# The hidden gradient for two slabs at a time, in matmuls of 512 columns, with the taps broadcast by quarters and a sixth gate/up tile

## The chip, the cores and the metric

The kernel runs on one core of a Trainium2 chip. Its time is the device time of one execution in microseconds (us). The engines are named as in the profile: PE is TensorE (PEld its weight loads), DVE is VectorE, ACT is ScalarE, POOL is GpSimd and SP is SyncE, which here only issues DMAs. Each engine works through its own queue in order; they wait for one another by semaphores.

## What is computed

Inputs are bf16: q, k, v and the incoming gradient of 2048 × 1024 (S × D), four shift taps a channel, a filter of 2048 taps a channel (ssm_k), and weights w_gate and w_up (1024 × 3584) and w_down (3584 × 1024). The forward part, cut to what matters:

```
xn = layernorm(q)
kv = shift(k, taps) * v
y  = irfft(rfft(kv) * rfft(ssm_k)) + kv * ssm_D
s  = xn * y
g  = silu(((xn @ w_gate) * (xn @ w_up)) @ w_down)
out = q + s * g
```

The kernel returns out and its gradients for q, k, v, the taps, ssm_k, ssm_D and the three weights. Two of the backward products matter below. With dbm the gradient of the down projection's result, the hidden gradient is dh = dbm @ w_downᵀ (2048 × 3584); it is multiplied by gate and by up, elementwise, to give the gradients of up and gate, and these give dw_gate and dw_up = xnᵀ @ (…).

## The kernel before

**Stages.** Up to about 500 us: the gate and up matmuls (line 671) with the forward convolution beside them. To about 700: the down projection (L1034) with the backward of the silu gate, row block by row block. From 700 to 1317: dh and dw, the stage that the change is about. Then the gradient of w_down (L1582) to 1506, and the gradient of xn (L1644) to the end.

**The dh/dw stage.** The 3584 hidden columns are cut in NSL = 14 slabs of SLW = 256. For one slab there are two half tiles (first and second 1024 rows), each a tile of 1 MB that holds gate and up for 8 row blocks of 128: `[P, a, b, f]` with a = gate/up, b = row block, f = 256 columns. `gu_in` (L1342) loads them from GUd; `U[(11, 6, 2, 3, 12)[k % 5]]` are the five rooms in which they go round. U is the list of large work tiles of 8 KB a partition.

- `dh_half` (L1471) computes dh for one half tile. For each of 8 row blocks it runs 8 matmuls of 256 columns (L1482, one for each dc, the 128-row piece of D), with w_downᵀ of the slab as the moving operand. Two row blocks share one psum tile of 512 columns; ScalarE copies it to `dht` (L1484). After four row blocks a `multiply` is put on the list todo: VectorE multiplies gate and up of four row blocks by `dht` in place. After the second the whole tile is stored to DGd.
- `dw_slab` (L1495) computes dw_gate and dw_up of one slab in 8 groups (dc), each 16 matmuls of 512 columns (L1499; the moving operand is 256 columns of gate and 256 of up), a copy to `wb` (L1504), and after each second group two stores. After each group it takes one step of `others`, which is dh of the next slab: four steps, behind the groups 0 to 3.
- `load_wdt` (L1328) loads w_downᵀ of a slab, by a transposing DMA on SP's queue, into a pool `bw` of two buffers; it is called behind group 3 for the slab after next.
- `after_group` runs what is on todo and then `btick`, which lets a pump issue the next piece of the convolution's backward part: VectorE, ScalarE and POOL work that is spread over the stage and its successors, in proportion to the matmuls issued.

**Order of queues.** The program's order within an engine is that of the calls, except that a scheduler may move an instruction that has no data wait ahead; `tc.issue_after` and PIN hold some in place. SP issues the loads of this stage (gate/up tiles, w_downᵀ, the h tiles and the DBM tiles for the next stage) and the stores of wb and DGd; POOL issues the convolution's transfers and, behind slabs 1 to 4, four transfers that add q to out in memory.

**The taps.** The four shift taps, broadcast to all partitions, are read by VectorE in the forward shift (`shift(dp)`, L759, for four quarters dp of 256 channels) and in the backward units `dk_units` (L1204, 16 units of 128 channels and half the rows) in the last stage. They lie in `Wbc`, a tile of 8 KB a partition that lives through the whole kernel. WTd is the transposed taps in memory. `st` and `cld` are helpers that issue a transfer on POOL's queue, `ld` one on SP's.

Of the kernel before, what the change touches and what calls it, by code (L numbers as in the profile page):

```python
# [13 lines left out]
BF16 = mybir.dt.bfloat16  # L14
# [5 lines left out]
def build_kernel(  # L20
# [11 lines left out]
    nc = tc.nc  # L32
# [92 lines left out]
    nc.scalar.activation(warm[:], warm[:], ACT.Sqrt)  # L125
    RSTD = const.tile([P, NB], F32, name="RSTD")
    RSTN = const.tile([P, NB], F32, name="RSTN")
    Wbc = const.tile([P, 4, D], BF16, name="Wbc")

    tip = tc.alloc_tile_pool(name="tip", bufs=1)  # L130
    TI = tip.tile([P, 2, 8, 2, P], BF16, name="TI")
# [9 lines left out]
    def load_bcast(bsb):  # L141

        wrow = bsb.tile([1, D, 4], BF16, name="wrow")
        st(wrow[:].rearrange("p d j -> p (d j)"), A_shift_k.rearrange("(o d) j -> o (d j)", o=1))
        wtap = bsb.tile([1, 4, D], BF16, name="wtap")

        def turn(j):
            nc.gpsimd.tensor_copy(wtap[:, j, :], wrow[:, :, j])

        def spread():  # L150
            st(WTd.rearrange("(o x) -> o x", o=1), wtap[:].rearrange("p j d -> p (j d)"))
            st(Wbc[:].rearrange("p j d -> p (j d)"), bass.AP(WTd.tensor, WTd.offset, [[0, P], [1, 4 * D]]))
        return turn, spread

    def angles(tg):
# [378 lines left out]
    Dz = kst.tile([P, D], BF16, name="Dz")  # L534
    V.memset(Dz[:], 0.0)
    krow = kst.tile([P, 2, 11, 256], BF16, name="k")
    V.memset(krow[0:1, 0, 0:3, :], 0.0)
    bsb = pool("bc_sb", 1)
    tg = pool("tg", 1)
# [200 lines left out]
    def conv_forward():  # L740
        S_ = conv_state

        def load_kv(dp, c):
            S_["k", dp] = krow
            if dp > 0 or c == 0:
                for i in range(2) if dp == 0 else (c,):
                    cld_k(krow[:, i], i, dp)
            if dp > 0 or c == 1:
                for i in range(2) if dp == 0 else (c,):
                    v = U[4][:, 2048 * i:2048 * i + 2048].rearrange("p (a x) -> p a x", a=8)  # L750
                    cld_v(v, i, dp * 256, 256)
# [6 lines left out]
        def shift(dp):  # L758
            kv = cx.tile([P, NB, 256], BF16, name="kv")  # L759
            S_["kvt", dp] = kv  # L760
            k = S_.pop(("k", dp))
            wb = lambda j: Wbc[:, j:j + 1, dp * 256:(dp + 1) * 256].unsqueeze(1).to_broadcast([P, 2, 8, 256])
            room = cx.tile([P, 16, 256], BF16, name="KX")[:].rearrange("p a x -> p (a x)") if dp == 0 else U[7][:]
            acc, prod, v = [t.rearrange("p (c r d) -> p c r d", c=2, r=8) for t in (U[6][:], room, U[4][:])]
            with tc.issue_after(last.ins):
                tt(acc, k[:, :, 0:8, :], wb(3), MUL)
            yield 2.3
            for j in (2, 1, 0):
                tt(prod, k[:, :, 3 - j:11 - j, :], wb(j), MUL)
# [300 lines left out]
    while conv_state["filters"]:  # L1070
        bm_first([fc_])
        fc_ += 1
    bw = pool("bw", 2, side="right")
    mh = [pool("mh0", 1, side="right")]
    ps_bx = pool("ps_bx", 1, space=PSUM)

# [127 lines left out]
    def dk_units(ew):  # L1204
# [9 lines left out]
        def load_turned(i):  # L1214
# [7 lines left out]
                nc.sync.dma_start_transpose(out=dkT[:], in_=DKSHd[ds, c * H:c * H + H, :])  # L1222
            return kT, dkT

        dk = load_rows(0)
        yield 3
        for i in range(16):
            ds, c = divmod(i, 2)
            dsl = slice(ds * P, (ds + 1) * P)
            wb = lambda j: Wbc[:, j:j + 1, dsl].to_broadcast([P, 8, P])  # L1230
            acc = ew.tile([P, 8, P], BF16, name="dka")
            tt(acc[:], dk[:, 3:11, :], wb(3), MUL)
            for j in (2, 1, 0):
# [92 lines left out]
            defer(turn)  # L1326

    def load_wdt(sl):  # L1328
        wdt = bw.tile([P, DC, SLW], BF16, name="wdt")
        wdt_ld[0] = nc.sync.dma_start_transpose(out=wdt[:], in_=B_w_down[sl * SLW:(sl + 1) * SLW, :])  # L1330
        return wdt

    def load_ht(bp):
        ht = mh[bp % 2].tile([P, NF, 256], BF16, name="ht")
# [1 line left out]
            last = ld(ht[:, f0:f1], ht_rows(bp, f0, f1))  # L1336
        return (lambda fc: ht[:, fc]), last

    DGU = {}
    wdts = []  # L1340
# [12 lines left out]
    room = [bw.tile([P, DC, SLW], BF16, name="wdt")[:].rearrange("p (i x) f -> p i (x f)", i=2) for i in range(2)]  # L1353
# [61 lines left out]
    for bp in range(2, 8):  # L1415
# [6 lines left out]
        with tc.issue_after(row_ld[0].ins):  # L1422
            if bp in (4, 5, 7):
                q = (4, 5, 7).index(bp)
                dma_t = nc.sync.dma_start_transpose(out=DBMT[q], in_=DBMd[512 * q:512 * q + 512, :])
            if bp == 6:
                wdts.append(load_wdt(0))
                dma_t = wdt_ld[0]
        with tc.issue_after(dma_t.ins) if dma_t is not None else nullcontext():
            rows_in[2 * bp + 1] = gate_rows(2 * bp + 1)  # L1430
        if bp > 5:
            with tc.issue_after(row_ld[0].ins):
                gu_in(0) if bp == 6 else wdts.append(load_wdt(1))
        for i in range(2):
            n = (2 * bp + i - 2) * NF
            while done < n + NF:
# [11 lines left out]

    XN = [u8(q, a=4) for q in (7, 0, 1, 9)]
    bg = pool("bg", 2, side="right")  # L1450
    U.append(bg.tile([P, 4096], BF16, name="U12", bufs=1))
    ps_b = ps_tr = pool("ps_b", 4, space=PSUM)
    tr_name[0] = "psb"
    ps_c3 = pool("ps_c3", 2, space=PSUM)
# [13 lines left out]
            todo.pop(0)()  # L1468
        btick(n)

    def dh_half(k, wdt):  # L1471

        sl, hf = divmod(k, 2)
        dgu = DGU[k]
        for g in range(2):
            dht = bg.tile([P, 4, SLW], BF16, name="dht", bufs=3)
            for e in range(2):
                ps = ps_b.tile([P, 512], F32, name="psb")
                for x in range(2):
                    b = 4 * g + 2 * e + x  # L1480
                    for dc in range(DC):
                        nc.tensor.matmul(ps[:, x * SLW:(x + 1) * SLW], DBMT[2 * hf + g][:, dc, (b % 4) * P:(b % 4 + 1) * P],  # L1482
                                         wdt[:, dc, :], start=(dc == 0), stop=(dc == DC - 1))
                nc.scalar.copy(out=dht[:, 2 * e:2 * e + 2].rearrange("p b f -> p (b f)"), in_=ps[:])  # L1484
# [45 lines left out]
    PIN[0] = PINQ[0] = True  # L1530
    for k in range(2):
        run(dh_half(k, wdts[0]))
    todo.pop()()
    for sl in range(NSL):
        if sl + 1 == NSL:
            load_h(0)
            for q in range(4):
                ld(DBM[q], DBMd[512 * q:512 * q + 512, :].rearrange("(b u) d -> u b d", u=P))
            load_h(1)

        def halves():
            for k in (2 * sl + 2, 2 * sl + 3):
                if k < 2 * NSL:
                    yield from dh_half(k, wdts[sl + 1])
# [263 lines left out]
```

## Time and profile before

| | |
|---|---|
| time, median of 3 runs (from to) | 1912.02 us (1911.76 to 1912.31) |
| the profiled execution, its time | 1911.63 us |
| its span in the profile | 1909.9 us |
| granted TensorE clock | 1.00 |
| dh, 1792 matmuls (L1482), first and last | 700.1 to 1273.6 us |
| transposing loads of w_downᵀ (14), issue, shortest/median/longest | 1.7 / 4.9 / 12.8 us |
| the same, issue to landing, shortest/median/longest | 4.2 / 9.3 / 21.7 us |
| gate/up tile load, 1 MB (28), issue to landing, median | 9.3 us |

A line of the group view reads: line, engine, operation, output and input, shape, count, busy time in us, mean in ns of one, and the idle time of the engine before them. A line of the waits view reads: engine and its instruction, the instruction waited for, then total us, number of waits and the longest. The profile's mean of a matmul (273 ns for 256 columns, 379 for 512) includes its pipelined end, which lies beside the next matmul.

### The profile page before, as it was taken

What the parts mean: (1) busy time and instruction counts of PE and PEld (TensorE: products, weight loads), DVE (VectorE), ACT (ScalarE), POOL (GpSimd) and SP (SyncE); (2) the same over time, 40 slices, a digit from 0 to 9 for tenths busy, and PEclk for the clock granted to TensorE, in tenths of its full rate; (3) what the DMA queues carried; (4) which work ended last, traced back from release to release, by engine and by line L of the source; (5) the groups of instructions that cost most, each with busy time, mean ns of one, the idle gap of its engine ahead of it and who ended that gap; (6) DMA issues with size and microseconds to landing.
All of it is one profiled execution on the core that took longest, in us unless ns stands there. A gap on an engine that the chain in (4) does not pass through costs nothing.

```text
span 1909.9 us, 28150 instructions
## 1 busy us (share of the span) xinstructions
PE 1899.4 (99%) x11379; PEld 1013.9 (53%) x11379; DVE 1549.7 (81%) x1711; ACT 636.8 (33%) x927; POOL 332.7 (17%) x465
## 2 busy tenths in 40 slices
PE   8999999999999999999999999999999999999999
PEld 5555555545444466666666665664444444444444
DVE  8999999999988556887999999999995305788862
ACT  5765555556333233432222222222222102111121
POOL 5121211201113220001031221211212101111120
PEclk9999999999999999999999999999999999999999
DMA  9777766769769997677897798585887999989852
GB/s 298 269 263 233 251 208 223 252 211 311 241 227 307 316 314 231 209 231 233 264 277 247 231 266 258 184 286 180 230 238 181 219 206 190 194 187 190 194 166 88
DMA packets 425106, 444.34 MB, mean 233 GB/s; under 512 B 268400, under 2 KB 342796, under 8 KB 410512
## 3 DMA queue, kind: packets, MB, share of 16 engines
q1 hardware_dynamic: 367504, 239.03, 45.9%
q0 software_dynamic: 41152, 174.15, 29.0%
q10 hardware_dynamic: 16320, 29.36, 4.1%
q8 instruction: 89, 1.46, 0.3%
q14 instruction: 41, 0.34, 0.1%
HBM read 193.87 MB, written 189.84 MB: 201 GB/s over the span
## 4 chain that ended last, share of the span: by engine, by line
PE 97%; DVE 1%; ACT 1%; DMA 0%; issue 0%; SPq 0%; ACTq 0%
PE psb L1499 20%; PE psx L1644 20%; PE psg L671 19%; PE psb L1482 10%; PE psbm L1034 10%; PE psb L1582 9%; PE psF L234 3%; PE psI L455 1%; PE tr L565 1%; PE psY L1193 1%; PE psY L445 1%; PE psx L1582 1%; DVE bst L578 0%; DMA wslab<-in_B_w_gate_dram 0%; PE tr L788 0%; DVE U L212 0%
## 5 line engine op out<-in xcount | busy, mean ns | idle before, releaser
L671 PE MATMUL psg<-wslab,U 128*128 128x512 bf16 x1792 | 401.8, 379 | 3.5 <-DMA wslab<-in_B_w_gate_dram 2.1
L1499 PE MATMUL psb<-U,U 128*128 128x512 bf16 x1792 | 397.1, 379 | 0.0
L1644 PE MATMUL psx<-U,dgut 128*128 128x512 bf16 x1536 | 332.8, 379 | 0.0
L1644 PEld LDWEIGHTS <-dgut 128*128 128x128 bf16 x1792 | 175.3, 98 | 211.4
L1499 PEld LDWEIGHTS <-U 128*128 128x128 bf16 x1792 | 175.2, 98 | 198.0
L671 PEld LDWEIGHTS <-U 128*128 128x128 bf16 x1792 | 172.6, 98 | 197.2 <-issue 3.6
L1482 PE MATMUL psb<-wdt,U 128*128 128x256 bf16 x1792 | 205.6, 273 | 0.0
L1482 PEld LDWEIGHTS <-U 128*128 128x128 bf16 x1792 | 175.2, 98 | 29.2
L212 DVE TENSOR_TENSOR W<-W 128x1024 f32<-128x1024 f32 (+1 forms) x189 | 186.5, 1003 | 4.1
L1582 PE MATMUL psb<-U,U 128*128 128x512 bf16 x816 | 177.3, 379 | 0.0
L1504 ACT CAST wb<-psb 128x512 bf16<-128x512 f32 x112 | 65.6, 586 | 315.4 <-PE psb L1499 310.5
L1249 DVE SCALAR_TENSOR_TENSOR dkp<-dkT,kT 128x1024 bf16<-128x1024 bf16 (+2 forms) x64 | 78.3, 1223 | 93.1 <-DMA dkT<-DKSHd 91.4
L1034 PE MATMUL psbm<-U,ht 128*128 128x512 bf16 x672 | 146.0, 379 | 0.0
L1582 PEld LDWEIGHTS <-U 128*128 128x128 bf16 x896 | 87.4, 98 | 104.4
L673 ACT CAST gut<-psg 128x512 bf16<-128x512 f32 x156 | 91.5, 589 | 120.2 <-PE psg L671 119.7
L1676 ACT ACTIVATE dx_t<-dxn 128x1024 bf16<-128x1024 f32 x15 | 15.9, 1057 | 324.7 <-DVE dxn L212 324.7
L1034 PEld LDWEIGHTS <-ht 128*128 128x128 bf16 x672 | 65.7, 98 | 78.1
L212 DVE TENSOR_TENSOR U<-U,dht 128x2048 bf16<-128x2048 bf16 x56 | 68.3, 1220 | 46.5 <-ACT dht L1484 46.5
L1484 ACT CAST dht<-psb 128x512 bf16<-128x512 f32 x112 | 65.6, 587 | 116.4 <-PE psb L1482 116.4
L66 POOL DMA_DIRECT2D Hd<-hN x54 | 36.6, 677 | 268.9 <-DVE hN L212 258.9
L1623 ACT CAST wbs<-psb 128x512 bf16<-128x512 f32 x51 | 29.9, 586 | 145.4 <-PE psb L1582 134.3
L212 DVE TENSOR_TENSOR W<-SP 128x1024 f32<-128x1024 f32 x64 | 74.1, 1218 | 1.3 <-ACT SP L295 0.8
(263 smaller groups left out, 2342.9 us busy)
## 6 DMA issues: line engine op xcount, KB each, us to landing
U<-GUd SPq DMA_DIRECT2D x28, 1024.0 KB, 9.3
DGd<-U SPq DMA_DIRECT2D x28, 1024.0 KB, 5.8
GUd<-gut ACTq DMA_DIRECT2D x39, 512.0 KB, 5.2
out_dram<-wb SPq DMA_DIRECT2D x112, 128.0 KB, 4.8
U<-Hd SPq DMA_DIRECT2D x14, 1024.0 KB, 6.6
Hd<-hN POOLq DMA_DIRECT2D x54, 256.0 KB, 4.5
HTd<-hT SPq DMA_DIRECT2D x24, 512.0 KB, 3.7
ht<-HTd SPq DMA_DIRECT2D x18, 512.0 KB, 7.5
```

Source lines behind the costliest of these rows:

```text
L212: pinned(V.tensor_tensor(o, a, b, op))
L234: mm = nc.tensor.matmul(ps[:, k].rearrange("p (c d) -> p c d", c=2), T[:, r, k, :], xr[:, r], start=(n == 0), stop=(n == len(rs) - 1 and ( ...
L671: gu_mm[0] = nc.tensor.matmul(ps[:], XNT[q][:, dc, qi * P:(qi + 1) * P], w[:, dc].rearrange("p a f -> p (a f)"), start=(dc == 0), stop=(dc ...
L673: nc.scalar.copy(out=gut[:, :, i], in_=ps[:].rearrange("p (a f) -> p a f", a=2))
L1034: mm = nc.tensor.matmul(ps[:, dh * 512:(dh + 1) * 512], ht(fc)[:, i * P:(i + 1) * P], WD[fc // 4][:, fc % 4, dh * 512:(dh + 1) * 512], sta ...
L1249: ins = V.scalar_tensor_tensor(prod[:].rearrange("p r d -> p (r d)")[:, lo:H], dkT[:, 0, lo:H], 1.0, kT[:, 0, 13 + m + lo:13 + m + H], op0 ...
L1482: nc.tensor.matmul(ps[:, x * SLW:(x + 1) * SLW], DBMT[2 * hf + g][:, dc, (b % 4) * P:(b % 4 + 1) * P], wdt[:, dc, :], start=(dc == 0), sto ...
L1484: nc.scalar.copy(out=dht[:, 2 * e:2 * e + 2].rearrange("p b f -> p (b f)"), in_=ps[:])
L1499: nc.tensor.matmul(ps[:], XN[b // 4][:, b % 4, dc * P:(dc + 1) * P], dgus[b // 8][:, :, b % 8], start=(b == 0), stop=(b == NB - 1))
L1504: nc.scalar.copy(out=wb[:, dc % 2].rearrange("p a f -> p (a f)"), in_=ps[:])
L1582: nc.tensor.matmul(ps, h[:, f, b, :], DBM[b // 4][:, b % 4, dh * 512:(dh + 1) * 512], start=(b == 0), stop=(b == NB - 1))
L1644: nc.tensor.matmul(ps[:, dh * 512:(dh + 1) * 512], t[n][:, f, i * P:(i + 1) * P], WGU[n][:, f, dh * 512:(dh + 1) * 512], start=(n == 0 and ...
```

## The change

dh is computed for a pair of slabs at once. A matmul has 512 columns, 256 of the one slab and 256 of the other, for one row block, so a psum tile holds one row block of two slabs, and a step of `dh_pair` ends after two psums. The steps of one pair are spread over two slabs of dw: behind groups 4 to 7 of the even slab for the first half of the rows, and behind groups 2 to 5 of the odd slab for the second. For the moving operand to reach both slabs with one stride, w_downᵀ lies in one tile `W3` with room for three slabs; behind group 5 of the odd slabs the loads of two slabs are issued one after the other (behind slab 0 one).

Since a pair needs its gate/up tiles earlier, a sixth room (`U13`, 8 KB) is added, and the rooms are handed out from a list. The 8 KB come from `Wbc`, which goes: a tile `WB` of 4 KB holds two quarters of the taps in the forward part (quarters 2 and 3 are loaded over the first two), and `wbk`, 2 KB in two buffers, one quarter in the backward units. `ho` shares the room of `vl`. The DBM tiles and the first h tile of the next stage are loaded one slab earlier, and a few loads around the start of the stage change places.

```diff
-    Wbc = const.tile([P, 4, D], BF16, name="Wbc")
...
-            st(Wbc[:].rearrange("p j d -> p (j d)"), bass.AP(WTd.tensor, WTd.offset, [[0, P], [1, 4 * D]]))
+            for dp in range(2):
+                load_taps(WB[:, dp], dp * 256, 256)
...
+    WB = kst.tile([P, 2, 4, 256], BF16, name="WB")
+
+    def load_taps(t, d0, w):
+        st(t, bass.AP(WTd.tensor, WTd.offset + d0, [[0, P], [D, 4], [1, w]]))
...
         def load_kv(dp, c):
             S_["k", dp] = krow
+            if dp > 1 and c == 0:
+                load_taps(WB[:, dp % 2], dp * 256, 256)
...
-            wb = lambda j: Wbc[:, j:j + 1, dp * 256:(dp + 1) * 256].unsqueeze(1).to_broadcast([P, 2, 8, 256])
+            wb = lambda j: WB[:, dp % 2, j:j + 1].unsqueeze(1).to_broadcast([P, 2, 8, 256])
...
-    bw = pool("bw", 2, side="right")
+    bw = pool("bw", 1, side="right")
+    W3 = bw.tile([P, 3, DC, SLW], BF16, name="wdt")
...
-        ho = ew.tile([P, 2, P, 8], BF16, name="ho")
+        ho = ew.tile([P, 2, P, 8], BF16, name="ho", tag="vl")
...
-            wb = lambda j: Wbc[:, j:j + 1, dsl].to_broadcast([P, 8, P])
+            if i % 4 == 0:
+                wbk = ew.tile([P, 4, 256], BF16, name="wbk", bufs=2)
+                load_taps(wbk[:], ds * P, 256)
+            wb = lambda j: wbk[:, j:j + 1, ds % 2 * P:(ds % 2 + 1) * P].to_broadcast([P, 8, P])
...
-    def gu_in(k):
-
-        if k < 2 * NSL:
-            t = U[(11, 6, 2, 3, 12)[k % 5]][:].rearrange("p (a b f) -> p a b f", b=8, a=2)
-            ld(t, GUd[k // 2, k % 2])
-            DGU[k] = t
+    gu_room = [11, 6, 12, 2, 13, 3]
+
+    def gu_in(sl, hf):
+
+        if sl < NSL:
+            DGU_U[sl, hf] = gu_room.pop(0)
+            DGU[sl, hf] = U[DGU_U[sl, hf]][:].rearrange("p (a b f) -> p a b f", b=8, a=2)
+            ld(DGU[sl, hf], GUd[sl, hf])
...
-    def dh_half(k, wdt):
-
-        sl, hf = divmod(k, 2)
-        dgu = DGU[k]
+    def dh_pair(p, hf):
+
+        if 2 * p >= NSL:
+            return
+        both = sorted((2 * p, 2 * p + 1), key=lambda sl: sl % 3)
+        lo, hi = [sl % 3 for sl in both]
         for g in range(2):
-            dht = bg.tile([P, 4, SLW], BF16, name="dht", bufs=3)
-            for e in range(2):
+            dht = bg.tile([P, 4, 2, SLW], BF16, name="dht", bufs=2)
+            for x in range(4):
                 ps = ps_b.tile([P, 512], F32, name="psb")
-                for x in range(2):
-                    b = 4 * g + 2 * e + x
-                    for dc in range(DC):
-                        nc.tensor.matmul(ps[:, x * SLW:(x + 1) * SLW], DBMT[2 * hf + g][:, dc, (b % 4) * P:(b % 4 + 1) * P],
-                                         wdt[:, dc, :], start=(dc == 0), stop=(dc == DC - 1))
-                nc.scalar.copy(out=dht[:, 2 * e:2 * e + 2].rearrange("p b f -> p (b f)"), in_=ps[:])
+                for dc in range(DC):
+                    nc.tensor.matmul(ps[:].rearrange("p (j f) -> p j f", j=2), DBMT[2 * hf + g][:, dc, x * P:(x + 1) * P],
+                                     W3[:, lo:hi + 1:hi - lo, dc, :], start=(dc == 0), stop=(dc == DC - 1))
+                nc.scalar.copy(out=dht[:, x].rearrange("p j f -> p (j f)"), in_=ps[:])
                 after_group(1)
+                if x == 1:
+                    yield
 
             def multiply(g=g, dht=dht):
                 bs = slice(4 * g, 4 * g + 4)
-                tt(dgu[:, :, bs], dgu[:, :, bs], dht[:].unsqueeze(1).to_broadcast([P, 2, 4, SLW]), MUL)
-                if g == 1:
-                    ld(DGd[sl, :, 1024 * hf:1024 * hf + 1024, :].rearrange("a (u b) f -> u a b f", u=P), dgu)
+                for j, sl in enumerate(both):
+                    dgu = DGU[sl, hf]
+                    tt(dgu[:, :, bs], dgu[:, :, bs], dht[:, :, j].unsqueeze(1).to_broadcast([P, 2, 4, SLW]), MUL)
+                    if g == 1:
+                        ld(DGd[sl, :, 1024 * hf:1024 * hf + 1024, :].rearrange("a (u b) f -> u a b f", u=P), dgu)
             todo.append(multiply)
             yield
...
             after_group(2)
-            if dc == 3 and sl + 2 < NSL:
-                wdts.append(load_wdt(sl + 2))
-            next(others, None)
+            if 0 <= dc - (2 if sl % 2 else 4) < 4:
+                next(others, None)
+            if dc == 5 and (sl % 2 == 1 or sl == 0):
+                for n in (sl + 4, sl + 5)[0:1 if sl == 0 else 2]:
+                    if n < NSL:
+                        load_wdt(n)
...
-    for k in (1, 2):
-        gu_in(k)
+    for k in ((1, 0), (0, 1), (1, 1)):
+        gu_in(*k)
+    load_wdt(2)
...
-    for k in (3, 4):
-        gu_in(k)
+    for k in ((2, 0), (3, 0)):
+        gu_in(*k)
...
-    for k in range(2):
-        run(dh_half(k, wdts[0]))
+    for hf in range(2):
+        run(dh_pair(0, hf))
     todo.pop()()
+    load_wdt(3)
     for sl in range(NSL):
-        if sl + 1 == NSL:
+        if sl + 2 == NSL:
             load_h(0)
...
+        if sl + 1 == NSL:
             load_h(1)
...
-        dw_slab(sl, [DGU[2 * sl], DGU[2 * sl + 1]], halves())
-        for k in (2 * sl + 5, 2 * sl + 6):
-            gu_in(k)
+        dw_slab(sl, [DGU[sl, 0], DGU[sl, 1]], dh_pair(sl // 2 + 1, sl % 2))
+        gu_room += [DGU_U[sl, 0], DGU_U[sl, 1]]
+        for k in ((sl + 2, 1), (sl + 3, 1)) if sl % 2 == 0 else ((sl + 3, 0), (sl + 4, 0)):
+            gu_in(*k)
```

More of the change, by code (lines that the diff above doesn't have):

```diff
@@ L1223, in load_turned @@
             return kT, dkT
+        wbk = None
         dk = load_rows(0)
@@ L1328, in load_wdt @@
     def load_wdt(sl):
-        wdt = bw.tile([P, DC, SLW], BF16, name="wdt")
-        wdt_ld[0] = nc.sync.dma_start_transpose(out=wdt[:], in_=B_w_down[sl * SLW:(sl + 1) * SLW, :])
-        return wdt
+        wdt_ld[0] = nc.sync.dma_start_transpose(out=W3[:, sl % 3], in_=B_w_down[sl * SLW:(sl + 1) * SLW, :])
     def load_ht(bp):
@@ L1337, in load_ht @@
         return (lambda fc: ht[:, fc]), last
-    DGU = {}
-    wdts = []
+    DGU, DGU_U = {}, {}
     wdt_ld = [None]
-    def gu_in(k):
-        if k < 2 * NSL:
-            t = U[(11, 6, 2, 3, 12)[k % 5]][:].rearrange("p (a b f) -> p a b f", b=8, a=2)
-            ld(t, GUd[k // 2, k % 2])
-            DGU[k] = t
+    gu_room = [11, 6, 12, 2, 13, 3]
[4 more added lines that the diff above has]
+            ld(DGU[sl, hf], GUd[sl, hf])
     with tc.issue_after(ht1[1].ins):
@@ L1352, in build_kernel @@
     bm_first(range(fc_, NF))
-    room = [bw.tile([P, DC, SLW], BF16, name="wdt")[:].rearrange("p (i x) f -> p i (x f)", i=2) for i in range(2)]
+    room = [W3[:, n].rearrange("p (i x) f -> p i (x f)", i=2) for n in range(2)]
     bms = [out_of(pss[i], room[0][:, i]) for i in range(2)]
@@ L1426, in build_kernel @@
             if bp == 6:
-                wdts.append(load_wdt(0))
+                load_wdt(0)
                 dma_t = wdt_ld[0]
@@ L1432, in build_kernel @@
             with tc.issue_after(row_ld[0].ins):
-                gu_in(0) if bp == 6 else wdts.append(load_wdt(1))
+                gu_in(0, 0) if bp == 6 else load_wdt(1)
         for i in range(2):
@@ L1450, in build_kernel @@
     bg = pool("bg", 2, side="right")
-    U.append(bg.tile([P, 4096], BF16, name="U12", bufs=1))
+    U += [bg.tile([P, 4096], BF16, name=f"U{i}", bufs=1) for i in (12, 13)]
     ps_b = ps_tr = pool("ps_b", 4, space=PSUM)
@@ L1538, in build_kernel @@
                 ld(DBM[q], DBMd[512 * q:512 * q + 512, :].rearrange("(b u) d -> u b d", u=P))
+        if sl + 1 == NSL:
             load_h(1)
[L1541 to L1544, printed above, removed]
-        dw_slab(sl, [DGU[2 * sl], DGU[2 * sl + 1]], halves())
-        for k in (2 * sl + 5, 2 * sl + 6):
-            gu_in(k)
+        dw_slab(sl, [DGU[sl, 0], DGU[sl, 1]], dh_pair(sl // 2 + 1, sl % 2))
+        gu_room += [DGU_U[sl, 0], DGU_U[sl, 1]]
+        for k in ((sl + 2, 1), (sl + 3, 1)) if sl % 2 == 0 else ((sl + 3, 0), (sl + 4, 0)):
+            gu_in(*k)
         if 0 < sl < 5:
```

## The prediction, made before the changed kernel ran

> **What bounds the kernel now.** I read the page first: busy time of each engine, the chain that ended last, the groups.
>
> ```profile
> PE 1899.4 (99%) x11379; PEld 1013.9 (53%) x11379; DVE 1549.7 (81%) x1711; ACT 636.8 (33%) x927; POOL 332.7 (17%) x465
> PEclk9999999999999999999999999999999999999999
> PE 97%; DVE 1%; ACT 1%; DMA 0%; issue 0%; SPq 0%; ACTq 0%
> L1499 PE MATMUL psb<-U,U 128*128 128x512 bf16 x1792 | 397.1, 379 | 0.0
> L1482 PE MATMUL psb<-wdt,U 128*128 128x256 bf16 x1792 | 205.6, 273 | 0.0
> L212 DVE TENSOR_TENSOR U<-U,dht x56: 1211/1219/1226, 707.4 to 1276.4; 128x2048 bf16<-128x2048 bf16 x56
> ```
>
> TensorE is busy for 99% of the span at the full granted clock, and 97% of the chain is its matmuls. What the edit touches is the stage from 700 to 1317 us: the dh matmuls (L1482), their multiplies on VectorE (the last line, from the view of tile dht), and the dw matmuls (L1499). So I then asked for that stage's row of the windows view, its waits, and its chain in order of time.
>
> ```profile
> 700.00:1317.00 617.00, 616.88 (x3947) 381.53 (x3945) 546.51 (x537) 185.08 (x303) 101.29 (x131) 1.00 0.77 244
> ...
> DVE U L212 <- ACT dht L1484: 46.5, 22, 5.7
> ...
> 714.64 3.45 PE psb L1499 x16
> 718.09 3.49 PE psb L1482 x32
> 721.58 3.45 PE psb L1499 x16
> ...
> 1273.89 31.08 PE psb L1499 x144
> ...
> 1505.88 386.77 PE psx L1644 x1792
> ```
>
> In the row the second number is the stage's length and the next five are the busy times of PE, PEld, DVE, ACT and POOL: TensorE 616.88 of 617.00, VectorE 546.51. No TensorE wait is listed in the stage. So the time can fall only by making matmuls shorter or fewer, and rise only by stopping TensorE, which VectorE or a late load can do. In the chain (start, length, what, count) 16 matmuls of 512 columns take 3.45 us and 32 of 256 columns take 3.49.
>
> **The change part by part.**
>
> *Wider dh matmuls.* 1792 matmuls of 256 columns become 896 of 512. The long pieces of the chain give the finest prices: 386.77/1792 = 215.8 ns for 512 columns (31.08/144 gives the same), and 6.99 us for the 64 of the first dh piece, 109.2 ns, for 256. Two narrow ones cost 2.6 ns more than one wide one; 896 × 2.6 = 2.3 us off the path. The group lines offer another price: 205.6 busy us for dh, and half of the 397.1 of twice as many wide matmuls is 198.5, a gain of 7.1. I don't take it: in the chain 112 groups × 3.453 = 387 us for dw, so the 397.1 holds some 10 us of ends that overlap the next matmul, and the same goes for the 205.6 against 56 × 3.493 = 195.6. But 7.1 stays as the upper bound of the gain. The new moving operand is two chunks of 256 columns from two slabs, and the new load of it costs nothing more: L1499 already reads two chunks, of the gate and up tiles, at 215.8 ns each.
>
> [...]
>
> *Casts and multiplies.* Before, each psum of two 256-column halves took one cast of 587 ns, 112 in all; after, each 512-column psum takes one, again 112. The multiplies keep their form, 56 of 1.22 us, but come in twos: 2.44 us in one place on VectorE, half as often. ScalarE has 185 us of work in 617 and VectorE the same total as before. Cost nothing in sum; the price is in the lateness of the second multiply, next.
>
> *The order of dh in the stage.* Before, dh of the next slab ended after group 3 of the slab's eight dw groups. After, the sixteen 512-column psums of a pair of slabs are spread, two at a stop, over the two slabs ahead of it: behind groups 4 to 7 of the even one and groups 2 to 5 of the odd one. The last stop of the pair stands behind group 5 of the odd slab. Then come groups 6 and 7 (6.9 us) and, in group 0 of the next slab, matmul 12 is the first to read the tile's last quarter, 2.6 us in. That is 9.5 us, less a cast (0.6) and two multiplies (2.44): 6.5 us in which VectorE may finish what it is at. Before, the same count with four groups and one multiply gives 13.8 + 2.6 − 0.6 − 1.2 = 14.6 us. VectorE pieces in its queue ahead of a multiply are 2.3 to 4.6 us long, and in the trace the time from the end of a cast to its multiply is under 6.5 us in 55 of 56 cases. The exception is this:
>
> ```profile
> 881.97 12.84 SPq L1330 DMA_TRANSPOSE wdt<-in_B_w_down_dram  x1
> ...
> 907.56 4.56 DVE L212 TENSOR_TENSOR m<-TF,B 128x4096 bf16<-128x4096 bf16 x3 [10.28 <-issue]
> ...
> 934.72 1.22 DVE L212 TENSOR_TENSOR U<-U,dht 128x2048 bf16<-128x2048 bf16 x1
> ```
>
> VectorE stood still for 10.28 us before 907.56 (the spectra came late, while a weight transpose held the SP queue 12.84 us), then worked off its queue, and the multiply at 934.72 came 10.56 us after its cast. Were that one to fall on one of the six transitions from an odd slab to an even one, TensorE would stop for 10.56 − 6.5 = 4 us. Lateness over 6.5 happened once in 56; for six transitions that makes 6/56, a tenth of a stop. I take 0 for the forecast and two stops, 8 us, for the upper bound.
>
> *The weight slabs.* A ring of three slabs in one buffer instead of two buffers; the transposes go out in twos behind group 5 of the odd slabs instead of one at a time behind group 3 of each. The first matmul that reads the new pair stands behind group 4 of the even slab: seven groups, 24 us later, against 9.3 us median and 21.7 at worst from issue to landing. Two in a row hold the SP queue for 2 × 1.7 to 2 × 12.8 us (median 4.9 each). Behind them stand the stores of wb and DGd and the loads of the gate and up tiles. Three wb buffers and four psums bridge 6 groups or 20.7 us. Expected cost 0; with both at the worst duration, 25.7 us, TensorE would wait some 2 to 5 us, once.
>
> *The gate and up tiles, six instead of five.* Their 28 loads of 1 MB are needed 24 us after an even slab's end and 31 us after an odd one's, and take 9.3 us median, 16.0 at worst in this stage. Nothing waited for them before, so the sixth room earns nothing by itself; it pays for the pairing. The loads of h and DBM one slab earlier also shorten no TensorE wait.
>
> *The taps.* One broadcast (852 ns of POOL issue, 7.5 us to landing, at 33.9 us) becomes two quarter loads there, two more with the k loads of quarters 2 and 3, and four in the dx stage, each about 0.9 us of POOL issue by that row. The first shift starts at 51.1, when VectorE waited 1.3 us for k and not for the taps; both quarters land by 45 even at double the time. Two extra issues delay k and v of quarters 2 and 3 by 0.9 us each on POOL, where VectorE is full (182.06 of 185 us between 100 and 285). TensorE waits for VectorE's kv once, for 0.6 us at 297; this may grow by the 0.9. In the dx stage (1506 to 1893) VectorE has 216 us of work in 387 and the first unit waits 26.7 us for dkh already, which covers the first loads. So from −0.6 (that wait gone) to +0.9; I take 0. The output tile ho now shares vl's room: vl is last read by the store issued at 1202.8, ho first written at 1234.8 (views of the two tiles), so neither waits.
>
> *Sum.* Profiled execution: 1911.63 us, of which 1909.9 are span and 1.7 lie around it, and 0.4 below the median of 1912.02. 1911.63 − 2.3 = 1909.3; on the median's level 1912.02 − 2.3 = 1909.7.
>
> **The rivals.**
>
> *The late second multiply decides (slower).* TensorE stops at the transitions from odd to even slabs because VectorE is more than 6.5 us behind. For it: the DMA share in this stage is already 0.77, two transposes now go in one burst with 1 MB gate and up loads and the four accumulating 1 MB transfers of out_0 (13.7 us median) in slabs 1 to 4, and the one starved stretch of before came from just this. Against it: only 1 of 56 multiplies was so late, and VectorE waited for its cast in 22 of 56, so it was ahead. It decides from a lateness of 6.5 us on; at two stops of 4 us: 1912.0 − 2.3 + 8 = 1917.7, at one stop 1913.7.
>
> *The gain is eaten (no change).* The pump's pieces fall at other places, the small waits of TensorE ahead of 300 us (nine in the waits view, 0.2 to 1.4 us each, 6.7 together) grow by one or two, and the 0.9 us at kv comes in: 1911 to 1912.5.
>
> *The busy sums are right.* The 7.1 us of the group lines: 1904.9. Against it the chain, whose pieces add up to the span without overlap.
>
> **How the numbers follow.** Forecast (1908.5 to 1911 in its own range, the 2.3 us ± about 1): 0.55. Gain eaten: 0.17. Stops: 0.22, of which 0.05 with a single one, under 1914, and a little past 1918. Busy sums: 0.06. A measurement of this kernel tells from no change about 0.2%, 3.8 us, so the forecast itself counts as no change. Faster by more than that: the busy sums and a little of the forecast's lower end, 0.09. Slower by more: the stops of two and more and half of the rest, 0.19. Same: 0.72. The range reaches from 1907 (half way into the busy sums' gap) to 1917 (nearly two stops).
>
> **What would show it.** Right: the dh group with 896 matmuls, pieces of 3.45 us for 16 in the chain, no TensorE wait between 700 and 1317, stage 2.3 us shorter; two transposes in a row on SP, each landing before 24 us. Stops: a wait of PE psb for DVE U about every 83 us in the stage (16 groups of dw and 16 psums of dh). Wrong altogether: dh pieces that take other than 3.45 us per 16, or TensorE waiting for the transposes of the weights.

## The result and the profile after

The changed kernel takes 1933.93 us (median of 4 runs, 1932.69 to 1935.05) against 1911.92 for the kernel before beside it: a ratio of 1.0115, 95% interval 1.0097 to 1.0132. It is 22 us slower where 2.3 us faster was forecast. The profiled execution took 1935.05 us, its span is 1933.3.

The lines of the page and of the views of the stage, as shown for the kernel before (L1492 is the dh matmul now, L1513 that of dw, L1518 the copy to wb):

```profile
PE 1897.3 (98%) x10345; PEld 928.0 (48%) x10483; DVE 1552.7 (80%) x1711; ACT 636.5 (33%) x927; POOL 337.4 (17%) x472
PEclk9999999999999999999998999999999999999999
PE 90%; DVE 4%; DMA 2%; issue 2%; ACT 1%; SPq 0%; POOL 0%; ACTq 0%; POOLq 0%; DVEq 0%
L1513 PE MATMUL psb<-U,U 128*128 128x512 bf16 x1792 | 397.2, 379 | 0.0
L1492 PE MATMUL psb<-wdt,U 128*128 128x512 bf16 x896 | 207.0, 386 | 16.9 <-ACT wb L1518 16.9
...
700.00:1317.00 617.00, 599.93 (x2933) 284.88 (x2932) 526.51 (x522) 179.41 (x294) 96.08 (x127) 0.98 0.77 241
...
ACT wb L1518 <- DMA out_dram<-wb: 39.7, 3, 21.8
...
PE psb L1492 <- ACT wb L1518: 16.9, 2, 11.0
```

TensorE now stands still inside the stage, twice, for 16.9 us together, and what ends both waits is the copy to wb, which itself waited for a store of wb to land. The granted clock of the stage is 0.98. The chain in order of time shows both stops (first the stop at 935 us, then that at 1032):

```profile
926.69 13.48 DMA out_dram<-wb
...
940.27 0.59 ACT wb L1518
940.86 0.04 issue
940.90 6.01 PE psb L1492 x16
946.91 3.45 PE psb L1513 x16
...
1024.84 16.93 DMA out_dram<-wb
...
1041.93 0.59 ACT wb L1518
1042.52 0.04 issue
1042.56 6.37 PE psb L1492 x16
1048.93 3.45 PE psb L1513 x16
```

A store of wb leaves at 926.69 and lands 13.5 us later; the copy and then the matmuls follow at once. ScalarE's timeline shows the last copy into the buffer that this store empties, done at 911.49, and the copy that had to wait until the buffer came free:

```profile
910.90 0.59 ACT L1518 CAST wb<-psb 128x512 bf16<-128x512 f32 x1 [2.82 <-PE psb L1513]
...
940.27 0.59 ACT L1518 CAST wb<-psb 128x512 bf16<-128x512 f32 x1 [14.97 <-DMA out_dram<-wb]
```

The first 16 matmuls behind each stop take 6.01 and 6.37 us instead of 3.45, because the granted clock had dropped to 0.50 (0.71 on average from 940 to 950 us; the last section has the rows). Why the store left so late, the timeline of SP's queue shows (start, duration of the issue, what):

```profile
903.99 19.73 SPq L1340 DMA_TRANSPOSE wdt<-in_B_w_down_dram  x2
923.81 0.53 SPq L61 DMA_DIRECT2D U<-GUd  x1
924.43 0.90 SPq L61 DMA_DIRECT2D DGd<-U  x2
925.42 1.99 SPq L61 DMA_DIRECT2D out_dram<-wb  x2
...
998.78 23.62 SPq L1340 DMA_TRANSPOSE wdt<-in_B_w_down_dram  x2
1022.49 1.11 SPq L61 DMA_DIRECT2D DGd<-U  x2
1023.70 5.10 SPq L61 DMA_DIRECT2D out_dram<-wb  x2
```

The two transposes in a row hold SP for 19.7 and 23.6 us. The stores of groups 6 and 7 wait behind them, and so do two gradient stores of 1 MB, which are then under way beside them: the DMA share is 1.01 from 923.8 to 940.2 us, against 0.77 in the stage.

The whole difference in the profiled execution, by where the last matmul ends (1929.52 against 1906.48, 23.0 us): the two stops 16.9; the half clock behind them (6.01 − 3.45) + (6.37 − 3.45) = 5.5; the start 2.0 (a wait for L675 that ended at 74.6 us ends at 76.6); one wait of 0.7 in the last stage; less the 2.3 us of the matmuls. That makes 22.8.

### The profile page after: what moved, and what is told of

It reads as the page before. It is cut to its first block, busy times and chain, and to the rows that moved or that the text cites. A ratio compares the mean times of both kernels' runs of the same rounds, so it can differ in the third digit from the quotient of the medians.

```text
span 1933.3 us, 26203 instructions
## 1 busy us (share of the span) xinstructions
PE 1897.3 (98%) x10345; PEld 928.0 (48%) x10483; DVE 1552.7 (80%) x1711; ACT 636.5 (33%) x927; POOL 337.4 (17%) x472
## 3 DMA queue, kind: packets, MB, share of 16 engines
q1 hardware_dynamic: 367504, 239.03, 46.5%
## 4 chain that ended last, share of the span: by engine, by line
PE 90%; DVE 4%; DMA 2%; issue 2%; ACT 1%; SPq 0%; POOL 0%; ACTq 0%; POOLq 0%; DVEq 0%
PE psx L1660 20%; PE psg L675 18%; PE psb L1513 16%; PE psbm L1040 10%; PE psb L1492 9%; PE psb L1598 9%; PE psF L234 3%; DMA out_dram<-wb 2%; PE psI L455 1%; DVE W L212 1%; PE tr L569 1%; PE psY L1200 1%; DVE m L212 1%; PE psx L1598 1%; DVE U L212 1%
## 5 line engine op out<-in xcount | busy, mean ns | idle before, releaser
L675 PE MATMUL psg<-wslab,U 128*128 128x512 bf16 x1730 | 399.1, 380 | 5.1 <-DMA wslab<-in_B_w_gate_dram 1.2
L1513 PE MATMUL psb<-U,U 128*128 128x512 bf16 x1792 | 397.2, 379 | 0.0
L1513 PEld LDWEIGHTS <-U 128*128 128x128 bf16 x1792 | 175.2, 98 | 207.8
L675 PEld LDWEIGHTS <-U 128*128 128x128 bf16 x1792 | 173.0, 98 | 196.5 <-issue 4.4
L1492 PE MATMUL psb<-wdt,U 128*128 128x512 bf16 x896 | 207.0, 386 | 16.9 <-ACT wb L1518 16.9
L1518 ACT CAST wb<-psb 128x512 bf16<-128x512 f32 x112 | 65.8, 587 | 336.9 <-PE psb L1513 295.3
L1492 PEld LDWEIGHTS <-U 128*128 128x128 bf16 x896 | 88.8, 99 | 123.8 <-issue 24.3
L1598 PEld LDWEIGHTS <-U 128*128 128x128 bf16 x896 | 87.3, 98 | 104.4
L212 DVE TENSOR_TENSOR U<-U,dht 128x2048 bf16<-128x2048 bf16 x56 | 66.0, 1220 | 46.4 <-ACT dht L1494 46.3
```

What stands on the lines that cost most here:

```text
L212: pinned(V.tensor_tensor(o, a, b, op))
L675: gu_mm[0] = nc.tensor.matmul(ps[:], XNT[q][:, dc, qi * P:(qi + 1) * P], w[:, dc].rearrange("p a f -> p (a f)"), start=(dc == 0), stop=(dc ...
L1492: nc.tensor.matmul(ps[:].rearrange("p (j f) -> p j f", j=2), DBMT[2 * hf + g][:, dc, x * P:(x + 1) * P], W3[:, lo:hi + 1:hi - lo, dc, :], ...
L1513: nc.tensor.matmul(ps[:], XN[b // 4][:, b % 4, dc * P:(dc + 1) * P], dgus[b // 8][:, :, b % 8], start=(b == 0), stop=(b == NB - 1))
L1518: nc.scalar.copy(out=wb[:, dc % 2].rearrange("p a f -> p (a f)"), in_=ps[:])
L1598: nc.tensor.matmul(ps, h[:, f, b, :], DBM[b // 4][:, b % 4, dh * 512:(dh + 1) * 512], start=(b == 0), stop=(b == NB - 1))
```

## The experiments

Each version was timed beside the kernel before, on the same chip, and its ratio is to that (in the three groups of runs the kernel before had medians of 1912.19, 1911.74 and 1912.15 us). A trace shows one execution of each version.

**One transpose at a time, first try (e1_single).**

```diff
-            if dc == 5 and (sl % 2 == 1 or sl == 0):
-                for n in (sl + 4, sl + 5)[0:1 if sl == 0 else 2]:
-                    if n < NSL:
-                        load_wdt(n)
+            if dc == 5 and sl + 4 < NSL:
+                load_wdt(sl + 4)
```

The second load of a pair is for the pair of slabs after the next one; it isn't needed for another 83 us, so that it can go out one slab later.

> The changed kernel with one edit: behind group 5 of every slab one transposing load of w_down (slab + 4), instead of two behind the odd slabs. The stops of TensorE (5.9 and 11.0 us, each followed by a stretch at half clock) come after two transposes in a row hold SP for 19.7 and 23.6 us, with the stores of wb behind them. Theory A (the pair of transposes is the cause: SP is held, the stores go late, the three wb buffers run out): no stop in the stage, and 1910 to 1912 us, the matmul gain of 2.3 being there, less up to 2 us at the start. Theory B (the transfers of the stage as a whole are too many at that point, with two 1 MB stores of DGd at once and the accumulation into out: the landing of the stores is late whatever SP does): the stops stay within half of their size, 1925 to 1935. Theory C (the late second multiply, the rival of the prediction): unchanged, 1934.

1930.31 us, ratio 1.0089 (1.0075 to 1.0103). The stops are there, 5.9 and 9.5 us. But the edit didn't do what it says, as SP's timeline of this run shows:

```profile
903.62 19.76 SPq L1340 DMA_TRANSPOSE wdt<-in_B_w_down_dram  x2
```

The load has no data to wait for, and the scheduler moved it back up to its neighbour. So this run tells nothing of taking the pair apart; it is in effect the changed kernel once more.

**The accumulations later (e3_acc_late).**

```diff
-        if 0 < sl < 5:
-            rows = slice(512 * sl - 512, 512 * sl)
+        if 7 < sl < 12:
+            rows = slice(512 * sl - 4096, 512 * sl - 3584)
```

> The changed kernel with one edit: the four accumulating transfers into out (1 MB each) go out behind slabs 8 to 11 instead of 1 to 4; the transposes stay in pairs. Theory A: the stops become smaller at most, since two transposes in a row still hold SP for 2 x 5 us or more ahead of the stores: 1915 to 1934. Theory B: no stop where they were, 1910 to 1914, unless new ones come with the accumulations in the later slabs. If the transposes of the pair take under 7 us each to issue now, the accumulations are what slows them, and the two theories are one cause in two parts.

1916.84 us, ratio 1.0021 (1.0012 to 1.0030). The first stop is gone, the second is 4.5 us; the first pair held SP for 13.4 us instead of 19.7. So the other traffic stretched the transposes, and a good part of the loss hangs on it. It isn't enough alone: the pair still stops TensorE where no accumulation is near.

**Narrow matmuls in the new order, and one tap load (e4_single_256, e7_single_taps1).** Both were built on e1_single and so carry the pair.

> As e1_single, and the dh matmuls have 256 columns again: per psum 8 for the one slab and 8 for the other, 1792 in all, everything else in the order of the changed kernel. By the prices of the chain (109.2 ns against 215.8) it is 2.3 us slower than e1_single; by the busy sums 7.1 us slower; 0 if the wide form with two chunks costs what two narrow ones do.

> As e1_single, and the first two quarters of the taps come in one load of 512 channels at the start instead of two of 256. In the changed kernel TensorE ran at half clock from 37.8 to 41.3 us, after short waits on VectorE, and the stage at 700 began 2.0 us later than before. If the second load on POOL's queue is the cause, this run starts the dh stage at about 700.2 us and is 2 us faster than e1_single, provided e1_single has the half clock; if it is the luck of the first load of q (VectorE waited 0.7 us for it at 18.7), the two are the same on the median and the half clock comes and goes among runs of both.

1926.15 us (ratio 1.0075, 1.0063 to 1.0088) and 1930.48 us (1.0092, 1.0077 to 1.0108). The narrow form came out faster than e1_single, which is no price of the width: its first stop was 0.3 us instead of 5.9, though the pair there held SP for 22.1 us, and why is not known. With stops of this size in the stage a price of 2 us can't be read. One tap load instead of two was the same on the median; the start is taken up below.

**One transpose at a time, pinned (e8_pinned).**

```diff
...
+            if dc == 5 and sl + 4 < NSL:
+                load_wdt(sl + 4)
+                tc.keep_in_program_order(wdt_ld[0])
```

> In e1_single the scheduler had moved the second transpose up to the first again (they stood at 903.6 and 917.9 us), so that run changed next to nothing. Here each of the loads is pinned to its place behind group 5 of its slab, and they stand 41 us apart on SP's queue. Theory A (two transposes in a row hold SP and load the DMA engines, the stores of wb go late): one transpose of about 14 us in the burst at 904 us remains, SP is free again at 918 instead of 924, the stop of 5.9 us goes to 0 and that of 11.0 to under 3: 1910 to 1916 us. Theory B (the burst of other transfers there decides): 1925 to 1934.

1911.12 us, ratio 0.9998 (0.9989 to 1.0007). SP's timeline and TensorE's waits in the stage:

```profile
903.05 14.49 SPq L1340 DMA_TRANSPOSE wdt<-in_B_w_down_dram  x1
917.63 0.53 SPq L61 DMA_DIRECT2D U<-GUd  x1
...
PE psb L1492 <- ACT dht L1494: 0.6, 1, 0.6
PE psb L1492 <- ACT wb L1518: 0.3, 1, 0.3
```

The loads now stand 30 to 54 us apart. The burst still stretches the single transpose to 14.5 us, but SP is free 6 us sooner; where the second pair held SP for 23.6 us, the two loads take 6.7 and 3.5 us, and 16.9 us of stops become 0.9. With the accumulations and the 1 MB transfers all in their places, taking the two apart removes the loss: theory A.

**The stores of wb on ScalarE's queue (e11_act), and with the pinned loads (e13_pin_act).**

```diff
-                    ld(dst[rows, fs].rearrange("(c p) f -> p c f", p=P), wb[:, :, a])
+                    sta(dst[rows, fs].rearrange("(c p) f -> p c f", p=P), wb[:, :, a])
```

> The changed kernel (transposes in pairs) with one edit: the stores of wb are issued by ScalarE, whose queue is free of transposes and 1 MB transfers, right behind the copy that fills wb. Theory A in the form that SP's queue is held: the stores leave in time, no wb wait, no stop: 1910 to 1914 us. Theory B in the form that any transfer lands late while the burst lasts (13 to 17 us after its issue): three wb buffers bridge 20.7 us, so a store that leaves in time and lands 17 us later does not stop TensorE either, but one that lands after 25 us does; then 1915 to 1925. If the loads or stores of the gate/up tiles are late by themselves, TensorE waits for these next, and the profile names them.

> e8_pinned and e11_act together: single transposes 41 us apart and the stores of wb on ScalarE's queue. All theories: if either alone has no stop, this has none: 1910 to 1912 us. A stop that is left here comes from the gate/up tiles or the multiplies, not from wb.

1917.19 us, ratio 1.0030 (1.0021 to 1.0040), and 1911.22 us, ratio 0.9996 (0.9987 to 1.0006). With the pair, one stop of 4.9 us is left, though SP's queue is out of the way. Two things still hold the stores. They land late, up to 22.6 us after their issue (6.2 in the median of the whole trace), though another engine issues them. And they left late after all:

```profile
1020.35 0.38 ACTq L72 DMA_DIRECT2D out_dram<-wb  x1
1020.84 1.07 ACT L1518 CAST wb<-psb 128x512 bf16<-128x512 f32 x2 [17.49 <-DMA wdt<-in_B_w_down_dram]
```

ScalarE stood still for 17.49 us ahead of these copies, and what ended this is the landing of a weight transpose, though the transpose was issued on SP's queue and the store that leaves just before them, at 1020.35, reads nothing of it. In the whole trace the copies to wb waited 24.5 us for transposes (two waits), 13.8 for stores of wb and 4.3 for a 1 MB gradient store. Why a store on ScalarE's queue waits for a transfer of SP's is not shown.

The median of e13_pin_act is as forecast, but the execution in its trace, the slowest of ten (1915.56 us), has a stop of 2.6 us by wb, which the expectation had ruled out. The pin holds a transpose in its place in SP's order, not in time: without the stores in that queue two transposes stood only 12 us apart (989.51 and 1001.26), and the second took 25.5 us to issue. The copy before the stop had waited 15.2 us, until a 1 MB gradient store landed.

**Finer buffers of wb (e10_wb6).**

```diff
-            if dc % 2 == 0:
-                wb = bg.tile([P, 2, 2, SLW], BF16, name="wb", bufs=3)
-            nc.scalar.copy(out=wb[:, dc % 2].rearrange("p a f -> p (a f)"), in_=ps[:])
-            if dc % 2 == 1:
-                fs, rows = slice(sl * SLW, (sl + 1) * SLW), slice((dc - 1) * P, (dc + 1) * P)
-                for a, dst in enumerate((o_dwg, o_dwu)):
-                    ld(dst[rows, fs].rearrange("(c p) f -> p c f", p=P), wb[:, :, a])
+            wb = bg.tile([P, 2, SLW], BF16, name="wb", bufs=6)
+            nc.scalar.copy(out=wb[:].rearrange("p a f -> p (a f)"), in_=ps[:])
+            fs, rows = slice(sl * SLW, (sl + 1) * SLW), slice(dc * P, (dc + 1) * P)
+            for a, dst in enumerate((o_dwg, o_dwu)):
+                ld(dst[rows, fs], wb[:, a])
```

> The changed kernel with one edit: wb is six buffers of one group (1 KB) instead of three of two groups, with two stores a group of 64 KB. A group's buffer is then free one group (3.45 us) earlier, for the same memory. If the depth of wb is what turns the late stores into stops, the two stops (5.9 and 11.0 us) lose about 3.5 us each, and the half clock behind the first goes: 1922 to 1930 us. If SP is short of issue time (112 stores of 0.4 us more in the stage), they stay or grow.

1912.15 us, ratio 1.0000 (0.9991 to 1.0010), and no wait of TensorE in the stage of its trace, though the pair stands as in the changed kernel and held SP for 18.2 us:

```profile
902.97 18.19 SPq L1340 DMA_TRANSPOSE wdt<-in_B_w_down_dram  x2
```

I had expected half of the stops to stay. In the same memory, a group's room comes free when its own store lands and not with its neighbour's. ScalarE still waited 31.1 us in all for wb, in 7 waits, but in pieces that the four psums bridge.

**Both, the start, the clean price of the width, and a control.** e14_pin_wb6 joins the pinned loads and the finer wb. e15_taps2k adds taps that lie in memory by quarters, so that a partition reads one run:

```diff
-        st(t, bass.AP(WTd.tensor, WTd.offset + d0, [[0, P], [D, 4], [1, w]]))
+        st(t, bass.AP(WTd.tensor, WTd.offset + 4 * d0, [[0, P], [1, 4 * w]]))
...
-            for dp in range(2):
-                load_taps(WB[:, dp], dp * 256, 256)
+            load_taps(WB[:].rearrange("p q j x -> p (q j x)"), 0, 512)
...
```

e17_256 is e15_taps2k with the dh matmuls narrow:

```diff
-                for dc in range(DC):
-                    nc.tensor.matmul(ps[:].rearrange("p (j f) -> p j f", j=2), DBMT[2 * hf + g][:, dc, x * P:(x + 1) * P],
-                                     W3[:, lo:hi + 1:hi - lo, dc, :], start=(dc == 0), stop=(dc == DC - 1))
+                for j, w in enumerate((lo, hi)):
+                    for dc in range(DC):
+                        nc.tensor.matmul(ps[:, j * SLW:(j + 1) * SLW], DBMT[2 * hf + g][:, dc, x * P:(x + 1) * P],
+                                         W3[:, w, dc, :], start=(dc == 0), stop=(dc == DC - 1))
```

e16_before_wb6 is the kernel before with the finer wb.

> The changed kernel with the transposes pinned one at a time (e8_pinned) and wb in six buffers of one group (e10_wb6). No stop in the dh stage in any execution; what then stays against the kernel before is the matmul gain of 2.3 us less about 1 us that the start loses before 76 us: 1910 to 1911.5 us, and less spread than either edit alone (10 runs: 1910.5 to 1914.4, and 1910.5 to 1913.6).

> As e14_pin_wb6, and the taps lie in memory by quarters, so that a load is one run of 2 KB (4 KB for the first two quarters, in one load) for each partition instead of four of 512 bytes. In the trace the four TENSOR_SCALAR of the layer norm at 34 us took 1.92 us before, 2.29 with one load of 4 x 128 pieces and 2.57 with two of them beside it on POOL; TensorE waits for these. If the count of pieces that POOL writes for a transfer is what slows VectorE there, they take 1.92 again and this run is 0.5 to 2 us faster than e14_pin_wb6 (2 where the half clock at 37 us goes too): 1908.5 to 1910.5 us. If not: the same as e14_pin_wb6.

> As e15_taps2k, and the dh matmuls have 256 columns again (two times 8 per psum, 1792 in all), everything else the same. Without stops on either side this is the clean price of the width: 2.3 us slower than e15_taps2k by the chain, 7.1 by the busy sums, 0 if two chunks of one wide matmul cost what two narrow ones do.

> The kernel before with wb in six buffers of one group. It has no stop in its dh stage (one wait of 2.9 us of ScalarE for wb, none of TensorE), so finer buffers should change nothing: within 0.1% of 1912. If it gains, wb was a limit before the change too, and the gain of e14_pin_wb6 is not the change's alone.

| | us, median (from to) | ratio, 95% interval |
|---|---|---|
| before | 1912.15 (1911.53 to 1916.33) | |
| e14_pin_wb6 | 1911.29 (1910.78 to 1915.41) | 0.9997 (0.9989 to 1.0006) |
| e15_taps2k | 1910.19 (1909.32 to 1913.42) | 0.9990 (0.9981 to 0.9999) |
| e17_256 | 1912.80 (1911.61 to 1917.72) | 1.0004 (0.9995 to 1.0013) |
| e16_before_wb6 | 1911.74 (1911.34 to 1913.58) | 0.9997 (0.9988 to 1.0005) |

None of the new-order kernels in this table has a TensorE wait in the stage of its trace. The width is worth 1912.80 − 1910.19 = 2.6 us on the medians. In the traces it is 2.3 us: from the first to the last copy to dht, 548.3 us pass narrow (e17_256, the first line) and 546.0 wide (e15_taps2k):

```profile
L1494 ACT CAST dht<-psb x112: 566/586/653, 703.6 to 1251.9; 128x512 bf16<-128x512 f32 x112
...
L1493 ACT CAST dht<-psb x112: 566/586/608, 703.3 to 1249.3; 128x512 bf16<-128x512 f32 x112
```

The finer wb alone gives the kernel before nothing that its interval shows. e15_taps2k is the one version faster than before by its interval, by 2.0 us on the medians. The smaller spread expected of e14_pin_wb6 did not show: two of its eleven executions took 1914.6 and 1915.4 us, with a mean granted clock of 0.998 and 0.999, and no trace shows where. The trace of e15_taps2k is of its slowest execution (1913.42 us), which has a wait of 2.0 us for VectorE in the last stage; the 40 matmuls behind it take 10.48 us, where 40 of 215.8 ns make 8.63.

The start: the four TENSOR_SCALAR of the layer norm on VectorE, in before, after and e15_taps2k in turn:

```profile
34.09 1.92 DVE L597 TENSOR_SCALAR U<-U,mv,RSTD 128x1024 bf16<-128x1024 bf16 x4
```

```profile
34.84 2.58 DVE L601 TENSOR_SCALAR U<-U,mv,RSTD 128x1024 bf16<-128x1024 bf16 x4
```

```profile
34.11 1.91 DVE L600 TENSOR_SCALAR U<-U,mv,RSTD 128x1024 bf16<-128x1024 bf16 x4
```

Two tap loads of 4 × 128 pieces beside them on POOL cost VectorE 0.66 us, in two of the four instructions (0.93 and 0.82 us instead of 0.55); with one such load (e7_single_taps1) one of them takes 0.93; with one piece a partition none does. TensorE's wait there goes 0.72, 1.10 and 0.33, and 0.73 us in the same order.

Not all of the 2.0 us that the changed kernel's start lost is due to the taps. In its trace the first load of q landed late, so that VectorE's first work on it began at 18.67 us instead of 17.94, ahead of any tap load. This moment differs from execution to execution (17.94 and 18.28 us in the two kernels with the old start), so this 0.7 us is chance. From it to the end of the wait at 74.6 or 76.6 us, 56.7 us pass in before, e16_before_wb6, e15_taps2k and e17_256, and 57.4 in e3_acc_late, e8_pinned, e11_act and e14_pin_wb6, which have two tap loads. Where a half clock follows (after, at 0.50 from 37.8 to 41.2 us, e4_single_256, e10_wb6, e13_pin_act), 57.8 to 58.0 pass. So the tap loads cost 0.7 us, and the half clock, where it comes, 0.4 to 0.6 more.

## Why the prediction was wrong

**Right.** The price of the width: 2.3 us by the chain, measured 2.3 in the traces and 2.6 on the medians; 16 wide matmuls take 3.45 us, and the 7.1 of the busy sums was an overlap. The moving operand of two slabs costs nothing extra. The sixth room earns nothing by itself: no TensorE wait for a gate/up tile in any run. The tap loads of quarters 2 and 3 were hidden: the wait at kv stayed 0.6 us.

**Wrong: the step on the weight slabs.** It priced the pair at "Expected cost 0; with both at the worst duration, 25.7 us, TensorE would wait some 2 to 5 us, once", by setting how long SP is held against the 20.7 us that wb and the psums bridge. The mechanism was named and its size was wrong. The first pair held SP for 19.7 us, less than the 20.7, and TensorE still stopped for 5.9. The runs show three reasons:

- The store behind the hold had to land as well. The room of wb was lost from the copy to the landing. For the store issued at 926.69, whose copy was done at 911.5, that was 28.7 us: 15.2 behind SP and 13.5 from issue to landing, in company with the two 1 MB gradient stores that were held with it. TensorE had work for 23.5 us from that copy on (911.5 to 935.0).
- Two slow loads in a row were priced as a rare case, with an expected cost of 0. The long single transpose of before (12.84 us) lay in a burst of the convolution's transfers (DMA share 1.01 from 882 to 895 us); in such a burst a pair was stretched as a whole. It happened twice, to 19.7 and 23.6 us (DMA share 1.06 and 1.16 meanwhile), which is inside the 25.7 that the step allowed for. The accumulations are part of the first burst (e3_acc_late).
- The stops cost more than their length. Behind each, 16 matmuls ran at half clock for part of the time, which cost 5.5 us together: a third on top.

The step also took both loads of a pair as needed 24 us later. One of them isn't needed for 83 us more, so nothing was to be had from issuing them together, as e8_pinned shows by taking them apart at no cost.

**Wrong: the rival on the slower side.** It looked for the stops where the accumulations load the DMA engines, in slabs 1 to 4, at the transition from an odd to an even slab, by the second multiply. They came in slabs 4 and 6, some 24 us behind the transition, by wb. VectorE was never what TensorE waited for in the changed kernel's stage, and it waited 46.3 us for the casts, as before (46.5). The rival's price, two stops of 4 us, was less than half of what came.

**Mis-sized: the taps.** The bounds of −0.6 to +0.9 us were set for POOL's queue and for the wait at kv. What came was VectorE slowed beside the issue at 34 us, 0.7 us on TensorE's path, and in some executions a half clock right behind it, 0.4 to 0.6 more. The other 0.7 us of the start is the late load of q, which is chance.

**Wrong, at no cost to TensorE: the room of ho.** The prediction says that neither ho nor vl waits. In the changed kernel POOL waits 7.7 us for a store of ho to land before it loads dkh for the first unit of the last stage, which it did not before, and this unit then waits 33.6 us, in the end for its taps, instead of 26.7 for dkh. TensorE did not wait for it.

**Open.** How much of the stretch of a transpose each neighbour in the burst causes was tried for the accumulations alone. The wait of 0.7 us in the last stage was not followed. Waits of TensorE for dxn of VectorE in that stage are in the traces of e1_single (1.2 us), e4_single_256 (0.8) and e15_taps2k (2.0), and in neither before nor e16_before_wb6; whether the later first unit is behind them is not shown.

## What to carry to other kernels

When a queue is held, set the whole life of the buffer behind it (from its copy to the landing of its store, under the traffic of that moment) against what bridges it, not the hold alone; then add a half clock that may follow a stop (here 5.5 us on 16.9 of stops). Two long issues that need not stand together should be pinned apart, since a scheduler may put a load that waits for nothing right back beside its neighbour, as it did here; and the trace must show that they stand apart in time, since a pin holds an order only. Several small buffers that come free one by one can be worth more than a few larger ones of the same memory (here 1912.15 us against 1933.93).

## What the runs showed of the hardware

**The clock.** At the changed kernel's stop of 5.9 us (935.0 to 940.9) the granted clock was 0.50 for 6.8 us, from 938.95 to 945.8, and at that of 11.0 us (1031.6 to 1042.6) for 13.7 us, from 1034.5 to 1048.2. So both times it fell inside the stop, 3.9 and 3.0 us after its start, and was back at 1.00 some 4.9 and 5.6 us after TensorE went on. In e3_acc_late, with one stop of 4.5 us, the mean clock of the traced execution was 0.999. The windows of the changed kernel around the first stop (length, then PE, PEld, DVE, ACT, POOL, the clock, DMA share and GB/s):

```profile
930.00:940.00 10.00, 5.03 (x24) 2.16 (x23) 9.86 (x11) 0.00 (x0) 0.00 (x0) 0.95 1.04 419
940.00:950.00 10.00, 9.10 (x32) 3.60 (x32) 4.96 (x6) 3.23 (x6) 0.00 (x0) 0.71 0.31 93
```

A stop inside the stage was not needed for it: at the start, the clock of the changed kernel was 0.50 for 3.4 us, from 37.8 to 41.2, behind two waits of L569 of 1.10 and 0.33 us that ended at 35.8 and 36.6. In e8_pinned and e10_wb6 these two waits were 1.1 and 0.3 us as well; the mean clock of the traced execution was 1.0 in the first and 0.999 in the second, which has no TensorE wait in the stage. One wait of 1.74 us at 24 us left the changed kernel's clock at 1.00 (20 to 37 us). How much idle time it takes, and what sets how long the half clock lasts, stays open.

**VectorE beside a transfer of POOL's.** A TENSOR_SCALAR of 128 × 1024 in bf16 went from 0.55 to 0.93 us while POOL issued a transfer of 4 × 128 pieces (after, e7_single_taps1), and stayed at 0.55 beside one of 128 pieces (before, e15_taps2k).
